# Seven buffers for phase products, halved stores of the last transform, reordered late tiles and W loads spread over the last group

## Chip, cores, metric

One core of one Trainium2 chip runs the kernel. The metric is the device time of one execution in microseconds (us).

## The reference, cut to what matters

```python
def reference(x, h, w_theta, w_tok_r, w_tok_i, w_ch):       # x: 8 x 5696 x 128
    y = irfft(rfft(x, 2 * S) * rfft(h, 2 * S))[:, :S]       # long convolution over the sequence
    theta = y @ w_theta
    zr, zi = y * cos(theta), y * sin(theta)                 # the phase products
    m = einsum('ts,bsd->btd', w_tok_r, zr) + einsum('ts,bsd->btd', w_tok_i, zi)   # W is 5696 x 5696, twice
    u = y + m
    return u + relu(u @ w_ch)
```

The first quarter of the kernel is the convolution, the rest the mixing over the sequence with the two large W matrices. This is about the **handover** between them.

## The kernel before

The convolution runs in eight groups, each in stages A to D. In the last group (stage C from about 408 us, stage D from about 440 us) the phase steps of the first batch half run beside it. The steps of the second half run beside the first mixing products. Each of the 22 steps of a half makes one tile of phase products:

```python
def phase_step(ti, hh):                        # tile ti, batch half hh
    for b in range(4):
        nc.tensor.transpose(tpz[:, b, :], yT[:, b, :], ident_bf)
    if hh:
        y_ap = st["sby"].tile([P, 4, D], BF16, tag="y", name="y_ap")   # 2, later 4 buffers
    else:
        ...                                                            # six slots of "ring"
    def copy():
        nc.vector.tensor_copy(y_ap, tpz)       # ... and a store of y_ap to y2_hbm
    phases_b(ti, y_ap, ...)
    ...
# in phases_b: cos and sin on ScalarE, two products on VectorE, then the stores
zz = fh.tile([P, 2, HD * CK], F16, tag="hs", name="zz")                # four buffers
zi_eng.tensor_mul(zi, red, yflat)
nc.vector.tensor_mul(zr, mag, yflat)
# second half: straight into the operand tiles b of the first mixing pass ("home"), or to z_hbm
(nc.gpsimd if e and r else nc.sync).dma_start(home[j]..., zz[...])
nc.sync.dma_start(z_hbm[...], zz[rows])
```

Of the 11 operand tiles of the first mixing pass, 0 to 8 are home tiles, filled straight from `zz`. Tiles 9 and 10 go through memory: products are stored to `z_hbm` and loaded again after the last step, when the convolution's buffers are free.

```python
def load_b(p, j, pool):
    t_ = tile_b(p, j, pool)
    for z in range(2):
        nc.scalar.dma_start(t_[:, z * 2048:(z + 1) * 2048]..., z_hbm[z, p, j]...)   # ScalarE's queue
```

The steps are called between the first mixing products, which also let further W loads go on GpSimd's queue (`upto` is how many W loads may have been issued, six to begin with):

```python
for q, (h, s) in enumerate(((0, 0), (0, 1), (1, 0), (1, 1))):
    for n in range(4):
        for j in range(TJ):
            product(...)
            if (n * TJ + j) % 2:
                next_steps(1)
        if n % 2 and q < 3:
            ring["upto"] += 1
            pump()
```

Of the kernel before, what the change touches and what calls it, by code (L numbers as in the profile page):

```python
# [22 lines left out]
def kernel(  # L23
# [288 lines left out]

    def stage_c(st):
        sg = sgn[:K1].unsqueeze(2).unsqueeze(1).to_broadcast([K1, 2, N2, 8])

        def chunk(q):
# [9 lines left out]
            g_in = ps[:K1].rearrange("p a (q r n) -> p r n (a q)", q=4, r=2)  # L326
            if q >= 64 and q % 16 == 0:
                nc.scalar.activation(g_out[:, :, :EN], g_in[:, :, :EN], AF.Copy)
                nc.scalar.mul(g_out[:, :, EN:], g_in[:, :, EN:], sgn[:K1, EN:EN + 1])
            else:  # L330
                nc.vector.tensor_tensor(g_out, g_in, sg, op=mult)
        return [lambda q=q: chunk(q) for q in range(0, 2 * HD, 8)]

    def stage_d(st, bp, dh, then=None):
        def chunk(n0, cn):
# [14 lines left out]
            if n0 + cn == N2:  # L350
                if then is not None:
                    then(yt)
                for e in range(2):
                    (nc.gpsimd if then else nc.sync).dma_start(yt_hbm[dh * HD:(dh + 1) * HD, 2 * bp + e, :],
                                                               yt[64 * e:64 * e + 64].rearrange("p m n -> p (m n)"))
        return [lambda n0=n0, cn=cn: chunk(n0, cn) for n0, cn in CHN]

    groups = [(bp, dh) for bp in range(B // 2) for dh in range(2)]

# [14 lines left out]
    def phases_b(ti, y_ap, b0, nb, yT, sb, th_pool, th_tag, zi_eng, turns=None, tags=("red", "mag"), m=P,  # L374
# [36 lines left out]
        if tags is None:  # L411
            zz = fh.tile([P, 2, HD * CK], F16, tag="hs", name="zz").bitcast(BF16)[:, :, :n]
            zr, zi = zz[:, 0], zz[:, 1]
# [7 lines left out]
        for e in range((m + 63) // 64):  # L421
# [7 lines left out]
            if tags is None and j in home:  # L429
                for r in range(2):  # L430
                    (nc.gpsimd if e and r else nc.sync).dma_start(
                        home[j][32 * i:32 * i + 32, :4096].rearrange("p (z q r n) -> p z q r n", z=2, q=2, r=2)[:, :, q_, r],
# [9 lines left out]
    chunks = [(p, tt, c) for p in range(2) for tt in pairs[p] for c in range(len(CHUNKS))]  # L442
    ring = {"n": 0, "read": set(), "wl": 0, "upto": 6}
    loaded = {}
# [57 lines left out]
    def open_phases():  # L502
        st = sides["phases"] = {}
        sb1 = pool("s2", 2, pha, reuse_waits="tile")
        sby = pool("s2y", 2, pha, reuse_waits="tile")
        st["sb1"], st["sby"] = sb1, sby
        sbc = pool("s2c", 1, pha, reuse_waits="tile")
# [40 lines left out]
    def phase_step(ti, hh):  # L548
# [11 lines left out]
        for b in range(4):  # L560
            nc.tensor.transpose(tpz[:, b, :], yT[:, b, :], ident_bf)
        if hh:
            y_ap = st["sby"].tile([P, 4, D], BF16, tag="y", name="y_ap")
        else:
            k = st["n0"] = (st.get("n0", 0) + 1) % 6
            y_ap = ring["all"][:, WB + 4096 + 512 * k:WB + 4608 + 512 * k].rearrange("p (b d) -> p b d", b=4)

# [11 lines left out]
    steps0 = [lambda ti=ti: phase_step(ti, 0) for ti in tile_order]  # L579

    for g, (bp, dh) in enumerate(groups):
        st = {}
        last = g + 1 == len(groups)
        a_, load_, b_ = front(g + 1)
        now = [steps0.pop(0) for _ in range(10)] if last else []
        c_ = stage_c(st)
        if dh == 0 and bp + 1 < B // 2:
# [67 lines left out]
    psp.close()  # L655
    sides["phases"]["sby"] = pool("s2y4", 4, pha, reuse_waits="tile")
    mps = ctx.enter_context(tc.tile_pool(name="mps", bufs=1, space=bass.MemoryType.PSUM, reuse_waits="tile"))
    steps1 = [lambda ti=ti: phase_step(ti, 1) for ti in tile_order]
    bp = cp = wlp = ybp = None
# [219 lines left out]
    for i, (k, p, tt, j0, s0, nj) in enumerate(stretches):  # L879
# [90 lines left out]
        if i == 1:  # L970
# [3 lines that stand above are left out]
                        product((held, a)[s], s * TJ + j, j, n, (h,))  # L974
                        if (n * TJ + j) % 2:
                            next_steps(1)
                    if n % 2 and q < 3:
                        ring["upto"] += 1
                        pump()
# [108 lines left out]
```

## Time and profile before

| | kernel before |
|---|---|
| median, range (4 runs) | 2150.63 us, 2147.27 to 2155.8 us |
| span of the profiled execution | 2155.9 us |
| last group: first product of stage C | 408.45 us |
| first product of stage D | 440.18 us |
| last phase product of the second half ends | 538.12 us |
| twelfth mixing result stored (to `cp_hbm`) | 650.73 us |

These four points cut the handover into three stretches. After the last of them both kernels do the same in the same order.

Timeline of before (columns: start, duration, engine, line and operation, in brackets the idle time before it and what ended it):

```profile
534.06 0.60 ACT L719 ACTIVATE ring<-tpz 128x512 bf16<-128x512 bf16 x1 [1.47 <-PE tpz L717]
540.77 3.42 ACTq L615 DMA_DIRECT2D b<-z_hbm  x4
```

```profile
549.04 3.57 PE L964 MATMUL m<-b,wt 128*128 128x512 bf16 x8 [3.39 <-DMA b<-z_hbm]
...
554.16 4.81 PE L964 MATMUL m<-b,wt 128*128 128x512 bf16 x12 [1.13 <-DMA b<-z_hbm]
```

The four loads stand behind L719, a copy that belongs to a background transposition. The copy is done at 534.7 us, the loads go out from 540.77 us, and TensorE waits 3.39 and 1.13 us for what they bring. Here the copy doesn't hold them: they leave 0.2 us after a store of phase products, issued at 538.15 us, has landed (540.56 us).

### The profile page before, as it was taken

What the parts mean: (1) busy time and instruction counts of PE and PEld (TensorE: products, weight loads), DVE (VectorE), ACT (ScalarE), POOL (GpSimd) and SP (SyncE); (2) the same over time, 40 slices, a digit from 0 to 9 for tenths busy, and PEclk for the clock granted to TensorE, in tenths of its full rate; (3) what the DMA queues carried; (4) which work ended last, traced back from release to release, by engine and by line L of the source; (5) the groups of instructions that cost most, each with busy time, mean ns of one, the idle gap of its engine ahead of it and who ended that gap; (6) DMA issues with size and microseconds to landing.
All of it is one profiled execution on the core that took longest, in us unless ns stands there. A gap on an engine that the chain in (4) does not pass through costs nothing.

```text
span 2155.9 us, 41270 instructions
## 1 busy us (share of the span) xinstructions
PE 2000.3 (93%) x15586; PEld 1124.8 (52%) x15765; DVE 1599.6 (74%) x2884; ACT 674.7 (31%) x992; POOL 889.7 (41%) x1628
## 2 busy tenths in 40 slices
PE   3788889768999999999999997999999999999998
PEld 3787888655444444444444443444444444444444
DVE  7766767766678888788876757578686868686867
ACT  5877868676123232323320000011111111111111
POOL 5211010215435454545556553353535353545351
PEclk8699879999999999999999999999999999999999
DMA  6356473888889998989999879587979797979784
GB/s 138 86 138 162 120 165 99 231 238 221 165 152 174 177 179 168 170 170 177 173 183 153 151 112 309 87 142 125 159 128 155 123 159 129 154 124 159 130 152 91
DMA packets 410695, 335.67 MB, mean 156 GB/s; under 512 B 85927, under 2 KB 361895, under 8 KB 409383
## 3 DMA queue, kind: packets, MB, share of 16 engines
q0 software_dynamic: 224544, 153.24, 50.8%
q1 hardware_dynamic: 178592, 166.02, 26.7%
q10 hardware_dynamic: 7360, 13.76, 1.8%
q8 instruction: 123, 2.02, 0.4%
q14 instruction: 76, 0.62, 0.1%
HBM read 377.11 MB, written 93.21 MB: 218 GB/s over the span
## 4 chain that ended last, share of the span: by engine, by line
PE 64%; DVE 3%; DMA 2%; issue 1%; ACT 0%; POOL 0%; DVEq 0%; ACTq 0%
PE m L1034 58%; PE m L964 2%; DMA b<-z_hbm 2%; DVE c L1041 1%; PE v L776 1%; PE utp L769 1%; PE m L1038 1%; DVE wt L689 1%; PE m L921 1%; PE m L919 1%; PE theta_ps L385 0%; PE tpz L717 0%; DMA yT<-yt_hbm 0%; DMA y_hbm<-ring 0%; POOL ring L493 0%
## 5 line engine op out<-in xcount | busy, mean ns | idle before, releaser
L493 POOL DMA_DIRECT2D ring<-in_moe_w_tok_i_dram x720 | 388.2, 547 | 686.2 <-DVE wt L689 612.1
L493 POOL DMA_DIRECT2D ring<-in_moe_w_tok_r_dram x720 | 386.8, 548 | 240.9 <-PE ps L211 103.5
L689 DVE STREAM_TRANSPOSE wt<-ring 128x384 f32<-128x384 f32 (+2 forms) x720 | 357.9, 522 | 116.3 <-PE m L1034 69.9
L1034 PE MATMUL m<-b,wt 128*128 128x512 bf16 x1604 | 386.6, 381 | 2.9 <-DVE wt L689 0.8
L1034 PEld LDWEIGHTS <-wt 128*128 128x128 bf16 x1804 | 176.6, 98 | 215.7 <-DVE wt L689 3.2
L1041 DVE TENSOR_TENSOR c<-c,m 128x512 f32<-128x512 f32 x412 | 265.1, 669 | 0.4 <-PE m L1034 0.4
L771 ACT ACTIVATE ring<-utp 128x512 bf16<-128x512 bf16 (+1 forms) x86 | 50.9, 592 | 608.6 <-PE utp L769 608.6
L323 PE MATMUL ps<-r_u,u_t 128*128 128x128 f16 x1024 | 133.9, 229 | 15.6 <-DVE u_t L307 12.8
L324 PE MATMUL ps<-r_v,v_t 128*128 128x128 f16 x1024 | 132.7, 228 | 0.0
L964 PE MATMUL m<-b,wt 128*128 128x512 bf16 x469 | 115.6, 393 | 11.4 <-DMA b<-z_hbm 5.8
L766 ACT ACTIVATE ub<-c 128x512 bf16<-128x512 f32 (+1 forms) x90 | 56.3, 628 | 199.1 <-DVE c L935 117.6
L129 POOL DMA_DIRECT2D x<-in_x_dram x64 | 34.1, 538 | 199.3 <-PE ps L193 187.7
L323 PEld LDWEIGHTS <-u_t 128*128 128x128 f16 x1024 | 106.5, 104 | 15.5 <-DVE u_t L307 15.5
L324 PEld LDWEIGHTS <-v_t 128*128 128x128 f16 x1024 | 105.5, 103 | 4.0 <-issue 2.5
L307 DVE TENSOR_TENSOR u_t<-xs,hs 128x1024 f16<-128x1024 f16 x96 | 69.8, 727 | 42.8 <-ACT xs L305 23.8
L305 ACT ACTIVATE xs<-ps 128x1024 f16<-128x1024 f32 x96 | 95.1, 1018 | 18.6 <-DVE v_t L307 10.9
L193 PE MATMUL ps<-f_t,x 89*128 89x180 f16 x512 | 85.0, 313 | 7.2 <-ACT xs L305 4.9
L964 PEld LDWEIGHTS <-wt 128*128 128x128 bf16 x528 | 51.4, 101 | 69.8 <-issue 17.0
L211 PEld LDWEIGHTS <-w_t 64*128 64x128 f16 x3240 | 64.6, 105 | 41.6 <-issue 27.2
L193 PEld LDWEIGHTS <-x 89*128 89x128 f16 x512 | 73.9, 236 | 9.3 <-issue 8.7
L387 ACT ACTIVATE red<-theta_ps,magic 128x512 f32<-128x512 f32 (+1 forms) x46 | 31.6, 687 | 133.5 <-PE theta_ps L385 113.5
L719 ACT ACTIVATE ring<-tpz 128x512 bf16<-128x512 bf16 (+1 forms) x46 | 27.4, 597 | 137.2 <-PE tpz L717 115.8
(2887 smaller groups left out, 3864.4 us busy)
## 6 DMA issues: line engine op xcount, KB each, us to landing
ring<-in_moe_w_tok_r_dram POOLq DMA_DIRECT2D x352, 96.0 KB, 4.5
ring<-in_moe_w_tok_i_dram POOLq DMA_DIRECT2D x352, 96.0 KB, 4.8
ring<-in_moe_w_tok_r_dram POOLq DMA_DIRECT2D x352, 80.0 KB, 4.4
ring<-in_moe_w_tok_i_dram POOLq DMA_DIRECT2D x352, 80.0 KB, 3.8
hs<-hf_hbm SPq DMA_DIRECT2D x192, 128.0 KB, 3.4
cp_hbm<-c SPq DMA_DIRECT2D x88, 256.0 KB, 2.3
c<-cp_hbm SPq DMA_DIRECT2D x88, 256.0 KB, 4.3
out_dram<-c SPq DMA_DIRECT2D x88, 256.0 KB, 4.3
```

What stands on the lines that cost most here:

```text
L193: nc.tensor.matmul(ps[:, i // 2, (i % 2) * 2 * K1:(i % 2 + 1) * 2 * K1], lhs(q + i), f1_t[:NB], start=True, stop=True)
L211: nc.tensor.matmul(ps[:, e, j * HD:(j + 1) * HD], w_t2[rows, c0 + j, N2 * (1 - ri):N2 * (3 - ri)], a_st["a"][rows, ri * K1 + c0 + j, :], s ...
L305: nc.scalar.activation(xs[:, :, :, :ck], ps, AF.Copy)
L307: nc.vector.tensor_tensor(uv[r][:, :, :, c0:c0 + ck], xs[:, :, :, :ck], hv[:, r:r + 1, :, :ck].to_broadcast([P, 2, HD, ck]), op=mult)
L323: nc.tensor.matmul(o, u_t[:, at:at + P], r_u, start=True, stop=False)
L324: nc.tensor.matmul(o, v_t[:, at:at + P], r_v, start=False, stop=True)
L493: nc.gpsimd.dma_start(wb[32 * i:32 * i + 32, :ng, :nj * 64], bass.AP(tensor=a.tensor, offset=a.offset + row0 * S + p * H + i * QR + j0 * 6 ...
L689: nc.vector.transpose(wt.rearrange("p j t r -> p (j t r)").bitcast(F32).rearrange("p (j g t) -> p g j t", j=TJ, g=4)[:, :ng, :nj], wb[:, : ...
L766: nc.scalar.activation(ub[:m].rearrange("p b d -> p (b d)"), c[:m], AF.Copy)
L964: nc.tensor.matmul(ms[n // 2 * 2 + h], a[n][:, j, :, r], bts_of[p][jj][n % 2 * 2 + h][:, r, :], start=(n % 2 == 0 and jj == 0 and r == 0), ...
L1034: nc.tensor.matmul(ms[q], a[q][:, j, :, r], bts[jj][q][:, r, :], start=(jj == 0 and r == 0), stop=(jj == NJ - 1 and r == 1 and q not in left))
L1041: nc.vector.tensor_tensor(c, z, ms[q], op=op)
```

## The change

Its intent is to take the waits out of the handover: more buffers for phase products, another division of their stores between queues, fewer bytes, an earlier start of what comes last. The diff, cut:

```diff
-            if q >= 64 and q % 16 == 0:                       # stage C: evictions on ScalarE
+            if q % 16 == 0 and (last or q >= 64):
...
-                    (nc.gpsimd if then else nc.sync).dma_start(yt_hbm[dh * HD:(dh + 1) * HD, 2 * bp + e, :],
-                                                               yt[64 * e:64 * e + 64].rearrange("p m n -> p (m n)"))
+                    t0 = H if then else 0                     # the last stores: second half only
+                    (nc.gpsimd if then else nc.sync).dma_start(
+                        yt_hbm[dh * HD:(dh + 1) * HD, 2 * bp + e, t0:],
+                        yt[64 * e:64 * e + 64].rearrange("p m n -> p (m n)")[:, t0:])
...
-            zz = fh.tile([P, 2, HD * CK], F16, tag="hs", name="zz").bitcast(BF16)[:, :, :n]
+            k = zz_n[0] = (zz_n[0] + 1) % (4 + ZB)            # ZB = 3: seven buffers
+            zz = (fh.tile([P, 2, HD * CK], F16, tag="hs", name="zz").bitcast(BF16) if k < 4 else
+                  sides["phases"]["zz"].tile([P, 2, 512], BF16, tag="zz", name="zz"))
...
-                    (nc.gpsimd if e and r else nc.sync).dma_start(
+                    (nc.gpsimd if r and (e or zz_n[0] % 2) else nc.sync).dma_start(
...
-    ring = {"n": 0, "read": set(), "wl": 0, "upto": 6}
+    ring = {"n": 0, "read": set(), "wl": 0, "upto": 0}
...                                                            # y_ap: six slots of ring in both halves
+    def with_load(step, load):                                # W loads spread over the last group
+        def both():
+            step()
+            if load:
+                ring["upto"] += 1
+                pump()
+        return both
...
-        now = [steps0.pop(0) for _ in range(10)] if last else []
+        now = [with_load(steps0.pop(0), 2 < n < 9) for n in range(10)] if last else []
...
-    steps1 = [lambda ti=ti: phase_step(ti, 1) for ti in tile_order]
+    steps1 = [lambda ti=ti: phase_step(ti, 1) for ti in
+              [0, 5, 11, 16, 1, 6, 12, 17, 10, 21, 2, 7, 13, 18, 3, 8, 14, 19, 4, 15, 9, 20]]
...
-                    if n % 2 and q < 3:
+                    if n % 2 and q == 1:                      # two calls in place of six
```

More of the change, by code (lines that the diff above doesn't have):

```diff
@@ L311, in stage_b, with stage_c @@
         return [lambda c=c: load(c) for c in range(LEAD)], [lambda c=c: chunk(c) for c in range(NCK)]
-    def stage_c(st):
+    def stage_c(st, last):
         sg = sgn[:K1].unsqueeze(2).unsqueeze(1).to_broadcast([K1, 2, N2, 8])
@@ L353, in chunk @@
                 for e in range(2):
-                    (nc.gpsimd if then else nc.sync).dma_start(yt_hbm[dh * HD:(dh + 1) * HD, 2 * bp + e, :],
-                                                               yt[64 * e:64 * e + 64].rearrange("p m n -> p (m n)"))
+                    t0 = H if then else 0
+                    (nc.gpsimd if then else nc.sync).dma_start(
+                        yt_hbm[dh * HD:(dh + 1) * HD, 2 * bp + e, t0:],
+                        yt[64 * e:64 * e + 64].rearrange("p m n -> p (m n)")[:, t0:])
         return [lambda n0=n0, cn=cn: chunk(n0, cn) for n0, cn in CHN]
+    zz_n, ZB = [0], 3
     groups = [(bp, dh) for bp in range(B // 2) for dh in range(2)]
@@ L504, in open_phases @@
         sb1 = pool("s2", 2, pha, reuse_waits="tile")
-        sby = pool("s2y", 2, pha, reuse_waits="tile")
-        st["sb1"], st["sby"] = sb1, sby
+        st["sb1"] = sb1
+        st["zz"] = pool("s2z", ZB, pha, reuse_waits="tile")
         sbc = pool("s2c", 1, pha, reuse_waits="tile")
@@ L561, in phase_step @@
             nc.tensor.transpose(tpz[:, b, :], yT[:, b, :], ident_bf)
-        if hh:
-            y_ap = st["sby"].tile([P, 4, D], BF16, tag="y", name="y_ap")
-        else:
-            k = st["n0"] = (st.get("n0", 0) + 1) % 6
-            y_ap = ring["all"][:, WB + 4096 + 512 * k:WB + 4608 + 512 * k].rearrange("p (b d) -> p b d", b=4)
+        k = st["n"] = (st.get("n", 0) + 1) % 6
+        y_ap = ring["all"][:, WB + 4096 + 512 * k:WB + 4608 + 512 * k].rearrange("p (b d) -> p b d", b=4)
         def copy():
@@ L584 @@
         a_, load_, b_ = front(g + 1)
-        now = [steps0.pop(0) for _ in range(10)] if last else []
-        c_ = stage_c(st)
+        now = [with_load(steps0.pop(0), 2 < n < 9) for n in range(10)] if last else []
+        c_ = stage_c(st, last)
         if dh == 0 and bp + 1 < B // 2:
@@ L655 @@
     psp.close()
-    sides["phases"]["sby"] = pool("s2y4", 4, pha, reuse_waits="tile")
     mps = ctx.enter_context(tc.tile_pool(name="mps", bufs=1, space=bass.MemoryType.PSUM, reuse_waits="tile"))
-    steps1 = [lambda ti=ti: phase_step(ti, 1) for ti in tile_order]
+    steps1 = [lambda ti=ti: phase_step(ti, 1) for ti in
+              [0, 5, 11, 16, 1, 6, 12, 17, 10, 21, 2, 7, 13, 18, 3, 8, 14, 19, 4, 15, 9, 20]]
     bp = cp = wlp = ybp = None
```

## The prediction

> **What bounds the kernel now.** I read the page first (engine shares, slices), then busy time in stretches of 10 us between 380 and 700 us, then the list of waits for 400 to 680 us, then the timelines of the sync queue, TensorE, VectorE, ScalarE and GpSimd there. The page says that TensorE bounds the kernel nearly everywhere, but that slices 8 to 10 (430 to 590 us; a slice is 53.9 us) are an exception in which the DMA engines are full:
>
> ```profile
> PE 2000.3 (93%) x15586; PEld 1124.8 (52%) x15765; DVE 1599.6 (74%) x2884; ACT 674.7 (31%) x992; POOL 889.7 (41%) x1628
> PE   3788889768999999999999997999999999999998
> DMA  6356473888889998989999879587979797979784
> ```
>
> The diff touches only this handover: the last transform group (about 408 to 457 us), the phase steps of the first batch half (412 to 475 us), those of the second half between the first mixing products (470 to 538 us), and the loads after them. The instruction orders confirm it: TensorE's is the same for its first 14,529 entries and its last 16,063, ScalarE's for its last 492, and GpSimd's differs only between its entries 133 and 207. From 650 to 1200 us TensorE is busy 99.4% or more, so whatever the handover gains moves the rest forward and stays in the total; nothing else can pay.
>
> By stretch (columns: stretch, length, busy TensorE, weight loads, VectorE, ScalarE, GpSimd, granted clock, DMA share, GB/s) TensorE loses time here:
>
> ```profile
> 460.00:470.00 10.00, 1.76 (x17) 1.09 (x16) 4.22 (x9) 5.67 (x11) 0.00 (x0) 0.81 0.99 223
> 470.00:480.00 10.00, 7.49 (x46) 4.68 (x48) 5.37 (x11) 5.24 (x9) 6.02 (x12) 0.68 0.96 289
> 480.00:490.00 10.00, 4.89 (x34) 3.06 (x35) 6.23 (x13) 4.59 (x8) 5.30 (x10) 0.83 1.04 386
> 520.00:530.00 10.00, 6.71 (x42) 3.80 (x41) 5.73 (x11) 6.04 (x11) 3.83 (x7) 0.71 0.77 194
> 540.00:550.00 10.00, 6.55 (x29) 2.85 (x28) 6.37 (x12) 0.00 (x0) 5.54 (x11) 0.91 1.07 238
> ```
>
> The waits (total, times, longest, in us) name the buffers and transfers behind that:
>
> ```profile
> ACT mag L407 <- DVE zz L418: 20.9, 9, 5.2
> DVE zz L417 <- DMA z_hbm<-zz: 14.8, 5, 5.7
> POOL b L626 <- DMA z_hbm<-zz: 13.1, 2, 12.7
> PE tpz L561 <- DMA ya<-yt: 6.9, 2, 5.4
> DVE y_ap L569 <- DMA y_hbm<-y_ap: 5.9, 3, 2.5
> PE m L964 <- DMA b<-z_hbm: 5.8, 4, 3.4
> ```
>
> VectorE waits for the stores of phase products (four buffers), ScalarE waits for VectorE, GpSimd waits for the same stores before it may load operand tiles, and TensorE waits for the transposed input. The sync queue shows why stores are late: it issues without a pause, and slows at the large transfers.
>
> ```profile
> 461.58 2.36 SPq L541 DMA_DIRECT2D ya<-yt  x1
> 464.05 4.92 SPq L435 DMA_DIRECT2D z_hbm<-zz  x2
> 479.45 1.94 SPq L435 DMA_DIRECT2D z_hbm<-zz  x2
> 495.33 27.67 SPq L431 DMA_DIRECT2D b<-zz  x38
> 401.37 2.21 POOL L493 DMA_DIRECT2D ring<-in_moe_w_tok_r_dram  x4 [103.54 <-PE ps L211]
> ```
>
> The first half's last product store is issued at 479 us, although its data stood ready at 475 us; 38 issues in 27.67 us are 0.73 us each.
>
> [...] 0.62 to 0.73 us an issue, three issues a step. [...] 0.68 granted at 470 to 480 us, after a gap of 5.42 us[...].
>
> **The change, part by part.**
>
> *W loads spread over the last group.* It does nothing, I expect. GpSimd has no instruction between the last input load and these 24 issues, in both orders, and the first one waits in both only for TensorE's last read of the old table (the 103.54 us in the last line above). Code that emits them later in the program doesn't make the queue wait. 0 us.
>
> *Half the evictions of the last transform stage on ScalarE.* Before, VectorE does 12 of 1.13 us (start to start) and 10 steps of 1.53 us (0.33 + 0.60 + 0.60): 28.9 us of the 29.6 between 410.6 and 440.2. After: 8 evictions, 24.3 us. ScalarE goes from 10 x 1.66 + 4 x 1.04 = 20.8 to 24.9 us. TensorE needs 16 x 0.90 + 10 x 1.10 = 25.4 us, plus 2 for its slow clock at the start: 27.4 us from 408.45. So TensorE becomes the limit and the next stage starts near 437.7 instead of 440.2: 2.5 us. That next stage is ScalarE's (7 evictions, 5.1 us, and 6 steps, 10.0 us, in 441.2 to 457.3) and only shifts.
>
> *Half of the last stores dropped.* The last two stores carry 64 x 5696 x 2 bytes each, 1.46 MB; now 64 x 2880, 0.74 MB. Between 457 and 472 us 3.29 MB moved at 219 GB/s, so 0.72 MB is 3.3 us. TensorE's wait for `ya<-yt` ended at 470.85; with the 2.5 us it ends near 465.0. Gain so far 5.8 us.
>
> *Seven buffers and six input slots.* From 470.85 to 488.8 us only 3 steps are finished; at the later pace of 2.2 us they take 6.6 us, so some 11 us are lost: VectorE's waits of 4.63 and 2.74 us for stores, TensorE's cold clock, and operand halves that load only once the stores are out. Seven buffers remove the two waits, 7.4 us; but TensorE then meets the operand loads, which must still land, so I count 6. From 488.8 to 522.5 us 15 steps take 2.2 us each, which is the sync queue's pace, 3 issues of 0.73 us. With three of seven buffers sending one more product through GpSimd it is 2.57 x 0.73 = 1.9 us, and TensorE becomes the limit: 1.10 us a step and its share of the 96 products, 96 x 0.216 / 22 = 0.94 us, 2.04 together. 15 x 0.16 is 2 us. The last four steps take 15.7 us (522.5 to 538.1) where 8.8 would do, with VectorE waiting 2.46 us for an input store and 1.56 us for a product store; with six input slots for four I count 4 of the 7.
>
> *Late tiles moved up.* Tiles 10, 21, 4 and 15 feed the two operands that pass through memory. TensorE's waits of 3.39 and 1.13 us for `b<-z_hbm` at 549 and 554 us should shrink by 3. But tiles 9 and 20 now come last and feed operands 7 and 8, which the next products need at once: a landing of about 4 us, less the 1.08 us waited there already, is partly in the open. Net 1 us.
>
> *W loads 8 and 9 later* (two fewer calls in the middle): 8 x 96 KB leave the crowded stretch; already in the above.
>
> Sum: 5.8 + 6 + 2 + 4 + 1 = 18.8 us. 2150.6 - 18.8 = 2131.8 us.
>
> **Rivals.** *DMA-bound.* The DMA share averages 0.92 from 400 to 540 us, with 32.9 MB at 235 GB/s. If bytes are the limit, more buffers only move the wait, and the gain is what leaves: 0.72 MB and 0.79 MB of W, 6.4 us: 2144 us. For it: shares near 1. Against it: other stretches move 289 and 386 GB/s, and shares of 0.70, 0.76, 0.77 and 0.53 (440 to 460, 520 to 540 us) show slack. *Full repair.* If the backlog of stores disappears, operand tiles come early too, all the lost 11 and 7 us return, and both waits for `b<-z_hbm` go: 5.8 + 11 + 2 + 7 + 4.5, about 30 us: 2120 us. *W late.* W loads 10 to 13 landed 14.5 us after their issue (538.8 to 553.3 us); if the phases end 18 us sooner but W takes as long and starts with two loads still open, the second tile pair waits up to 5 us (my estimate): 2137 us. Or the sums of operand 0, which overwrite the input slots, hold VectorE for the last input stores.
>
> **Range and chances.** The rivals span 2120 to 2144 us, and I take that as the range, with the sum of the parts in its middle. A gain over 2% needs 43 us; TensorE's idle time in the stretches from 410 to 570 us adds up to 32 us, so hardly 2 in 100. A loss of 43 us has no mechanism here.
>
> **What would show it.** Right: no wait of VectorE for `zz` stores before the second half's steps; `ya<-yt` ending near 465 us; first half's last product store issued before 472 us; about 2.05 us a step in the middle; the W loads still first issued at about 401 us; the stretch from 700 us on unchanged but shifted by about 19 us. Wrong: W issued later; DMA share at 1 with the same waits under other names; a new long wait of TensorE for `b<-zz` or W after the last step.

The 2 us for a slow clock at the start of stage C are an estimate from TensorE's timeline: the granted clock is 0.55 from 408.45 to 411.94 us and 1.00 from there to 420 us. "TensorE's cold clock" is the 0.68 granted at 470 to 480 us. "A landing of about 4 us" is that of the home stores, whose median from issue to landing is 4.2 us on the sync queue and 4.1 us on GpSimd's (405 to 560 us).

## More of the kernel before

A run that is one look only has one time, so I compare such runs by landmarks inside their profiles and not by their times.

Busy time in the stretches of before (columns: stretch, length, busy TensorE, its weight loads, VectorE, ScalarE, GpSimd, each with its number of instructions, then the clock granted to TensorE as a share of full speed, the busy share of the DMA engines, and GB/s):

```profile
408.45:440.18 31.73, 27.13 (x391) 24.36 (x397) 28.56 (x42) 21.31 (x38) 8.13 (x15) 0.95 1.08 276
440.18:538.12 97.94, 75.20 (x705) 49.69 (x719) 62.49 (x117) 65.10 (x111) 40.74 (x74) 0.90 0.88 228
538.12:650.73 112.61, 103.52 (x490) 47.73 (x499) 81.18 (x151) 27.92 (x46) 42.96 (x80) 0.92 0.82 159
```

Length minus busy TensorE is its idle time: 4.60, 22.74 and 9.09 us, together 36.4 us. That is all that a better handover could give, beyond a faster clock.

## The result

| | before | changed |
|---|---|---|
| median (4 runs each) | 2150.63 us | 2147.85 us |
| range | 2147.27 to 2155.8 us | 2143.98 to 2149.52 us |
| ratio, 95% interval | | 0.9982, 0.9958 to 1.0007 |
| span of the profiled execution | 2155.9 us | 2147.7 us |

A ratio is the mean time of one kernel's runs over that of the other's of the same rounds, so it isn't quite the ratio of the medians. The class is "same", as predicted. The time isn't: 2147.85 us lies above the range of 2120 to 2144 us.

In the page's slices (TensorE, DMA) of the changed kernel, counted from 0, TensorE's weakest slice (8, about 430 to 483 us) has risen from 6 to 7, and slice 10 (537 to 590 us) has fallen from 9 to 8:

```profile
PE   4788889778899999999999998999999999999998
...
DMA  6356473889779898999999879686969696879684
```

Of the stretches that the prediction showed, these answer in the changed kernel:

```profile
460.00:470.00 10.00, 4.42 (x33) 3.05 (x32) 8.62 (x17) 8.15 (x15) 3.14 (x6) 0.66 0.99 235
...
480.00:490.00 10.00, 6.44 (x54) 3.90 (x54) 5.38 (x10) 5.49 (x10) 6.88 (x13) 0.97 1.00 340
...
540.00:550.00 10.00, 5.79 (x18) 2.12 (x17) 1.68 (x4) 1.17 (x2) 3.46 (x7) 0.70 0.89 210
```

The head of the second half is better filled (4.42 and 6.44 us busy against 1.76 and 4.89), but 540 to 550 us is worse: 5.79 against 6.55 us, at a lower granted clock (0.70 against 0.91), and now the phase steps are long over there. The waits between 436 and 560 us (total, times, longest):

```profile
ACT ring L729 <- PE tpz L727: 13.4, 1, 13.4
...
DVE zz L422 <- ACT red L411: 12.8, 21, 1.4
...
PE m L974 <- DMA b<-z_hbm: 8.7, 4, 4.2
...
DVE ring L641 <- DMA y_hbm<-ring: 5.8, 1, 5.8
DVE ring L571 <- DMA y_hbm<-ring: 5.8, 3, 3.3
```

VectorE no longer waits for stores of phase products (14.8 us before) but for ScalarE, step by step. Its wait for the stores of transposed inputs (L571, the former L569) is as large with six slots as before (5.8 and 5.9 us); it now lies at 478 to 488 us and no longer at 508 to 525. TensorE's wait for operand tiles through memory has grown from 5.8 to 8.7 us. The wait in the first line has grown from 1.5 us. L641 is new: VectorE builds sums in the memory of the input slots and waits 5.8 us for their last stores, as the prediction's last rival said it might. No wait of TensorE behind it shows in this profile. The sync queue and GpSimd's first W loads in the changed kernel:

```profile
460.39 1.95 SPq L546 DMA_DIRECT2D ya<-yt  x1
...
474.55 1.81 SPq L440 DMA_DIRECT2D z_hbm<-zz  x2
...
498.43 16.41 SPq L436 DMA_DIRECT2D b<-zz  x22
```

```profile
398.93 2.21 POOL L498 DMA_DIRECT2D ring<-in_moe_w_tok_r_dram  x4 [101.41 <-PE ps L211]
```

The first half's last product stores went out from 474.55 us instead of 479.45; the predicted 472 was not reached. The queue still needs 16.41 / 22 = 0.75 us an issue. The W loads start as early as before, not spread at all.

The three stretches of the changed kernel:

```profile
407.54:437.72 30.18, 26.92 (x390) 24.28 (x397) 23.87 (x37) 25.62 (x46) 7.63 (x14) 0.94 1.08 277
437.72:521.05 83.33, 69.97 (x691) 47.83 (x704) 62.95 (x118) 64.96 (x110) 41.21 (x76) 0.92 0.90 246
521.05:641.65 120.60, 106.28 (x505) 48.50 (x514) 81.34 (x151) 28.53 (x47) 45.59 (x86) 0.94 0.83 158
```

Up to the last phase product it gains 1.55 + 14.61 = 16.2 us; then it gives 7.99 us back. Over all, 242.3 us have become 234.1. TensorE's idle time by stretch is 3.26, 13.36 and 14.32 us, together 30.9 instead of 36.4. The third stretch is where it got longer, by 5.2 us. The rest of what is given back is 2.8 us of TensorE's work, 15 recorded matmuls (490 and 505), that stood before the last phase product and now stand behind it.

What fills the third stretch is told by ScalarE's timeline of the changed kernel, then TensorE's:

```profile
532.36 0.60 ACT L729 ACTIVATE ring<-tpz 128x512 bf16<-128x512 bf16 x1 [13.35 <-PE tpz L727]
532.58 9.42 ACTq L625 DMA_DIRECT2D b<-z_hbm  x4
```

```profile
526.19 5.91 PE L974 MATMUL m<-b,wt 128*128 128x512 bf16 x18 [2.10 <-DMA b<-zz]
531.94 0.39 PE L727 MATMUL tpz<-ident_bf,yT 128*128 128x128 bf16 x4
...
538.52 1.89 PE L974 MATMUL m<-b,wt 128*128 128x512 bf16 x7 [2.10 <-DMA b<-z_hbm]
...
545.90 5.19 PE L974 MATMUL m<-b,wt 128*128 128x512 bf16 x12 [4.21 <-DMA b<-z_hbm]
```

The copy L729 waits 13.35 us for its transposition L727. That stands in TensorE's stream behind mixing products which wait for a home tile until 526.19 us. The four loads of tiles 9 and 10 stand behind the copy in ScalarE's queue, and the first two leave as soon as it has started. The last two (538.91 and 541.63 us) are held by something else, which act_order below shows; TensorE's longer wait, until 545.90 us, is for the third. So the phase steps end 17.1 us sooner (521.05 against 538.12), but the first of these loads goes out only 8.2 us sooner, and TensorE waits for them twice, 6.3 us in all, where it waited 4.5 us before.

### The profile page after: what moved, and what is told of

The parts are those of the page before. It is cut to its first block, busy times and chain, and to the rows that moved or that the text cites. A ratio compares the mean times of both kernels' runs of the same rounds, so it can differ in the third digit from the quotient of the medians. Undisturbed runs are those within 1.5% of the kernel's fastest.

```text
span 2147.7 us, 41283 instructions
## 1 busy us (share of the span) xinstructions
PE 1996.8 (93%) x15587; PEld 1121.7 (52%) x15765; DVE 1595.9 (74%) x2880; ACT 677.4 (32%) x1000; POOL 892.7 (42%) x1634
## 4 chain that ended last, share of the span: by engine, by line
PE 61%; DMA 3%; DVE 2%; issue 1%; POOL 1%; ACT 0%; DVEq 0%; ACTq 0%; POOLq 0%
PE m L1044 55%; PE m L974 2%; DMA b<-z_hbm 2%; POOL ring L498 1%; DVE c L1051 1%; PE v L786 1%; PE utp L779 1%; PE m L1048 1%; DMA ring<-in_moe_w_tok_r_dram 1%; DMA wl<-in_moe_w_tok_i_dram 1%; DVE wt L699 1%; PE m L931 1%; PE m L929 1%; DMA ring<-in_moe_w_tok_i_dram 0%; PE tpz L727 0%
## 5 line engine op out<-in xcount | busy, mean ns | idle before, releaser
L729 ACT ACTIVATE ring<-tpz 128x512 bf16<-128x512 bf16 (+1 forms) x46 | 27.4, 597 | 152.1 <-PE tpz L727 130.3
```

## The experiments

I made 18 more runs, two of them repeats: the twelve of the first three batches and six more because the cause was still open. The measure is the time between landmarks, in us. "C to D" is from the first product of the last group's stage C to the first of stage D, "D to product" from there to the end of the last phase product, "to result 12" from there until the twelfth mixing result is stored, and "whole" is the sum. "D to product" repeats within 1.6 us in the two pairs of equal kernels, "whole" within 2.8 us, so a difference in "whole" below 3 us says nothing. Each row is one profile.

| kernel | C to D | D to product | to result 12 | whole |
|---|---|---|---|---|
| before | 31.7 | 97.9 | 112.6 | 242.3 |
| before_again | 32.9 | 96.4 | 110.2 | 239.5 |
| changed | 30.2 | 83.3 | 120.6 | 234.1 |
| after_again (changed) | 30.6 | 82.6 | 118.8 | 232.0 |
| act_order | 30.0 | 83.8 | 115.9 | 229.7 |
| load_pool | 30.0 | 84.0 | 111.6 | 225.6 |
| four_bufs | 33.2 | 85.4 | 123.3 | 241.9 |
| full_store | 30.0 | 87.9 | 123.8 | 241.7 |
| dve_evict | 32.2 | 82.3 | 120.1 | 234.7 |
| old_order | 31.1 | 82.6 | 118.8 | 232.5 |
| no_split | 31.0 | 82.9 | 117.5 | 231.4 |
| four_nosplit | 31.0 | 88.1 | 115.6 | 234.7 |
| four_nosplit_slots4 | 30.4 | 85.9 | 117.3 | 233.6 |
| old_order_pool | 30.2 | 82.7 | 112.1 | 225.0 |
| pump3 | 31.4 | 83.8 | 114.0 | 229.3 |
| before_pump1 | 32.2 | 91.3 | 110.0 | 233.4 |
| before_half | 32.3 | 92.1 | 110.5 | 234.8 |
| before_half_pump1_pool | 32.6 | 88.4 | 108.5 | 229.5 |
| pump3_pool | 30.1 | 85.7 | 115.1 | 230.8 |
| before_pool | 33.0 | 97.6 | 105.6 | 236.1 |

My first theory after the result was **L**: what is given back comes from the late loads of tiles 9 and 10. The rival **R** was that something else binds there (the DMA engines, or a granted clock like the 0.70 of 540 to 550 us).

### after_again and before_again: how much is scatter

No edit; both kernels once more.

> The changed kernel once more, unaltered, for a ratio from more rounds and a second profile. In the first pair of profiles the changed one ends 8.1 us sooner, but the timed medians differ by 2.8 us only. Theory A: the 8.1 us are the change's and the first timing hid them in scatter; then the ratio comes out near 0.996 (8 us). Theory B: the first profile of the kernel before was a long execution (its run took 2157.6 us against a median of 2150.6); then the ratio is near 0.9985 (3 us), and a second profile of before will be shorter by several us outside the handover. In both the span from the start of the last group's stage D to the last phase product of half 1 is 83 us, and the stretch from there to the start of the fourth ScalarE copy of the first pair's results is 30 us.

> The kernel before once more, one look, for a second profile. By theory A its landmarks repeat within 1 us (last phase product of half 1 at 538 us, fourth copy of the first pair at 560 us, end at 2156 us). By theory B the last phase product still lies 97 to 98 us after the start of stage D of the last group, but the end is at 2147 to 2152 us, and the shift against the first profile arises gradually or in a place that has nothing to do with the handover.

after_again: median 2146.23 us of 6 runs (2139.11 to 2158.77) beside 2153.73 us of 11 runs of before; ratio 0.9975, interval 0.9949 to 1.0001. By the means the change is worth 2153.3 - 2147.5 = 5.7 us here and was worth 3.8 us in the first runs. The handover says 240.9 - 233.1 = 7.8 us, from two profiles each. Both theories of the expectation were too simple. The handover's gain does repeat. But before's second span is 2149.5 us against 2155.9: its stage C began 1.75 us sooner, its handover took 2.8 us less and the rest 1.8 us less. That is scatter spread over the whole execution, which is as large as the effect.

### act_order: ScalarE in program order at the head of the mixing

```diff
-            ordered.enter_context(tc.manual_schedule(engines={mybir.EngineType.DVE}))
+            ordered.enter_context(tc.manual_schedule(engines={mybir.EngineType.DVE} | ({mybir.EngineType.Activation} if p == 0 else set())))
```

> The changed kernel with ScalarE kept in program order over the first stretches of the mixing, so that the four loads of operand tiles 9 and 10 stand directly behind the last phase step in ScalarE's queue, ahead of the copy of a background transposition for which they wait 13.35 us in the changed kernel. Theory L (the 9 us given back after the last phase product are the late loads of tiles 9 and 10): the loads are issued at 522 to 529 us, the TensorE waits of 2.10 and 4.21 us on them at 538 and 546 us are gone or below 1 us, the fourth copy of the first pair starts at 543 to 547 us in place of 551.4, and the end moves by 5 to 8 us against the changed kernel, ratio to before 3 us lower or more. Rival R (the products after the last phase step are bound by something else: by the transfer engines, which the W loads fill, or by the cold clock): the loads go out sooner but land only 1 to 2 us sooner, and the end moves by less than 2 us.

Median 2141.64 us, ratio 0.9951 (0.9932 to 0.9969). ScalarE's and TensorE's timeline:

```profile
522.66 14.39 ACTq L625 DMA_DIRECT2D b<-z_hbm  x4
```

```profile
540.97 1.89 PE L974 MATMUL m<-b,wt 128*128 128x512 bf16 x8 [2.35 <-DMA b<-z_hbm]
...
544.20 1.02 PE L974 MATMUL m<-b,wt 128*128 128x512 bf16 x4 [1.34 <-DMA b<-z_hbm]
```

The first load went out 9.9 us sooner, and the copies of the first pair's results (four in all) began at 545.48 instead of 551.35 us, as L expected of what it calls the fourth; the mean time fell from 2147.5 to 2142.3 us. (With six runs each, and 2139.11 to 2158.77 us in the changed kernel, that difference alone isn't clear of scatter.) But the waits didn't vanish (3.7 us are left), because the four loads took 14.39 us to leave the queue. L holds in direction, and R's bound of 2 us is passed.

What spaced the four loads out is in the packed trace, which keeps the semaphores that each instruction waits for and each transfer reports on. In this program the transfers of the sync queue and of ScalarE's queue share eight semaphores (111 to 118; in the changed kernel 1,052 and 28 transfers report on them), and those of GpSimd's queue have eight of their own (101 to 108; 1,596 transfers). Each of these loads first waits until the last transfer on its semaphore has landed. Loads 2, 3 and 4 left at 528.59, 532.78 and 536.69 us, right after transfers of the sync queue had landed on theirs: a home store at 528.57 us, and two loads of `yT` for the background at 532.61 and 536.67 us, issued 9.6 and 12.8 us before. In the changed kernel the third and fourth load leave at 538.91 and 541.63 us in the same way, after the store of the copied tile (landed on semaphore 117 at 538.74 us) and a load of `yT` (on 118 at 541.61 us). So the copy holds two of the four loads, and transfers that have nothing to do with tiles 9 and 10 hold the others.

### load_pool: the same loads on GpSimd's queue

```diff
-            nc.scalar.dma_start(
+            (nc.scalar if p else nc.gpsimd).dma_start(
                 t_[:, z * 2048:(z + 1) * 2048]...
```

> The changed kernel with the loads of operand tiles 9 and 10 issued from GpSimd's queue instead of ScalarE's, everything else as it is. It tests theory L in another way, for ScalarE's order stays as it is. Theory L: the loads no longer wait for the ScalarE copy; they are issued when their data are there (522 to 529 us) unless W loads in front of them in that queue hold them, and the end moves by 3 to 8 us. Rival R: less than 2 us. If the W loads in front hold them the loads go out after 530 us, the gain is nil, and the run tells nothing against theory L.

Median 2143.67 us, ratio 0.9958 (0.9939 to 0.9976). GpSimd's timeline:

```profile
525.43 3.19 POOL L625 DMA_DIRECT2D b<-z_hbm  x4 [0.56 <-DMA ring<-in_moe_w_tok_i_dram]
```

All four loads left in 3.19 us, on GpSimd's semaphores, TensorE has no wait for them any more, and "to result 12" is 111.6 us, as short as before's. The whole handover is 7.5 us shorter than the changed kernel's mean of 233.1. So the late loads are shown in two ways. But this edit also takes them off the semaphores of the sync queue, and before_pool below shows that not all of its gain is the release from the copy.

### four_bufs, full_store, dve_evict, old_order: one part undone

```diff
-    zz_n, ZB = [0], 3
+    zz_n, ZB = [0], 0                      # four_bufs (its pool of three goes too)
-                    t0 = H if then else 0
+                    t0 = 0                 # full_store
-            if q % 16 == 0 and (last or q >= 64):
+            if q >= 64 and q % 16 == 0:    # dve_evict
-              [0, 5, 11, 16, 1, 6, 12, 17, 10, 21, 2, 7, 13, 18, 3, 8, 14, 19, 4, 15, 9, 20]]
+              tile_order]                  # old_order
```

> The changed kernel with four buffers for the phase products again in place of seven, all else as changed. Judged by the span from the start of the last group's stage D to the last phase product of half 1, which repeats within 1.5 us (97.9 and 96.4 us in two profiles of before, 83.3 and 82.6 in two of the changed kernel). Theory of the prediction (seven buffers give 6 us in the start transient, 2 in the middle and some of the last four steps): 90 to 94 us, and VectorE again waits for stores of phase products. Rival (the buffers are worth little once the W loads and the large stores are out of the way, so most of the 14 us is the half stores' and the queue split's): below 86 us.

> The changed kernel with the whole of the last transform's tiles stored again, all else as changed. Theory of the prediction (the half stores free the queues in front of the second half's first loads: 3.3 us): stage D to last phase product is 86 to 87 us instead of 83, and TensorE waits for the second half's operand (ya from yt) again. Rival (hidden): within 1 us of 83.

> The changed kernel with the evictions of the last group's stage C as before (VectorE alone in its first half), all else as changed. Theory of the prediction: the span from the first product of the last stage C to the first of stage D is 32.2 us (31.7 and 32.9 before; 30.2 and 30.6 changed), so 2 us longer, and the rest stays: 83 us from stage D to the last phase product. Rival: the 2 us are taken up by the waits at the head of the second half, so stage D to the last phase product shrinks by as much as stage C grows.

> The changed kernel with the second half's steps in the old order (tiles 10 and 21, which operand tiles 9 and 10 need, last again). Theory L (in the changed kernel the loads of operand tiles 9 and 10 stand behind a ScalarE copy until 532 us anyway): the new order is worth next to nothing there, so last phase product to fourth copy of the first pair stays at 30 us, within 3. Rival (the order is worth the 3 us and more that the prediction gave it): 33 us or more from the last phase product to that copy, and the loads wait for the stores of the phase products.

**four_bufs** took 85.4 us from stage D to the last product. That is below 86, so the rival is right there: three more buffers are worth 2.5 us there, though VectorE does wait 10.5 us for `zz` stores again. (Its stage C took 2.8 us longer too, 3.0 us of VectorE's waits there being for `zz` stores; the two other runs with four buffers don't show that, 31.0 and 30.4 us.) **full_store** took 87.9 us, a little more than the predicted 86 to 87, and TensorE waits 4.1 us for `ya` again: the half stores are worth some 5 us in that stretch. **dve_evict** added 1.8 us to stage C, and the next stretch was 0.6 us shorter than the changed kernel's mean; the theory of the prediction holds in size (TensorE waits for `ya` in this run too, 5.0 us, so that wait alone doesn't tell the store's effect). **old_order** came out at 232.5 us, like the changed kernel. The number is what theory L expected, but the run doesn't test its reason: here the scheduler put the copy behind the loads, and the first load left at 534.57 us, when the store of a late tile's products, issued at 527.52 us, had landed (534.55 us). Late data and a free queue came to the same as early data and a blocked one; old_order_pool below is the cleaner test.

Two wholes, 241.9 and 241.7 us, are larger than these parts explain. In both the copy stands ahead of the loads and the loads begin at 532.2 and 536.1 us, but so it does in dve_evict (532.0 us), whose whole is 234.7 us. In no_split, four_nosplit, four_nosplit_slots4, old_order and pump3 the scheduler put the copy behind the loads. The same edit thus also moves that copy, and a whole that differs by a few us can't be put down to the edited part alone.

### no_split, four_nosplit, four_nosplit_slots4: the buffer part undone piece by piece

```diff
-                    (nc.gpsimd if r and (e or zz_n[0] % 2) else nc.sync).dma_start(
+                    (nc.gpsimd if e and r else nc.sync).dma_start(        # in all three
# four_nosplit: ZB = 0 as well; four_nosplit_slots4: the pools of two and four for y_ap as well
```

> The changed kernel with every second product's store on the sync queue again (seven buffers, but the old division: one of four home stores on GpSimd, three on sync), all else as changed. Theory S (the pace of the middle steps, 2.2 us before and 1.97 us changed, is the sync queue's three issues of 0.73 us): the middle steps take 2.15 to 2.25 us again, whatever the number of buffers, and stage D to last phase product is 86 to 88 us in place of 83. Rival B (the seven buffers carry the pace by themselves): 1.97 us a step and 83 to 84 us.

> The changed kernel with four buffers and the old division of the stores, all else as changed. Four buffers alone gave 85.4 us from stage D to the last phase product, against 83. If the division and the buffers each take their own wait away, this one is about 89 us (83 + 2.5 + 3.5). If they stand in for each other (slow issues only hurt because four buffers run out), it is well above 90 us, near the 96 to 98 us of before.

> The changed kernel with the whole buffer part undone: four buffers for phase products, old division of their stores, and the transposed inputs of the second half in the old pools of two, later four, in place of six slots. Left of the change: evictions, half stores, order of the late tiles, two fewer W loads in the middle. By the prediction (buffers, slots and division 12 us of its sum) stage D to last phase product is 93 to 97 us. If it is 3 us or more above the run with four buffers and the old division, the six slots carry that; if it is equal, the slots are worth nothing.

no_split kept the pace of 1.97 us a step (from 502 to 514 us) and 82.9 us: theory S, that the sync queue's issue time sets the pace, fell. four_nosplit took 88.1 us, near the 89 of independent waits. With the slots undone as well it took 85.9 us, far below the 93 to 97 that the prediction implies. Its three stretches, last two rows:

```profile
438.44:524.31 85.87, 69.94 (x688) 48.11 (x701) 62.61 (x117) 65.62 (x111) 40.38 (x73) 0.90 0.90 240
524.31:641.58 117.27, 105.61 (x507) 48.78 (x517) 81.38 (x151) 28.54 (x47) 43.50 (x81) 0.96 0.82 162
```

TensorE's idle time over the handover is 3.1 + 15.9 + 11.7 = 30.7 us, the same as with everything (30.9 and 31.2). Buffers, slots and division together are worth 2.9 us up to the last product (116.3 against a mean of 113.4) and nothing to the twelfth result (233.6 against 233.1). In these three runs the copy stands behind the loads, and the first load leaves at 530.9, 528.2 and 528.4 us. The third still leaves only at 535.2 to 539.0 us, after loads of `yT` on the shared semaphores have landed, and TensorE waits 4.4, 7.8 and 7.5 us for the loads. Taking the copy away is thus not enough. The six slots were not undone alone beside seven buffers; no run shows that case.

That the pace was never the queue's can be read off the middle stretch, before and then changed:

```profile
490.00:515.00 25.00, 24.79 (x214) 15.54 (x217) 18.59 (x34) 19.01 (x34) 18.73 (x34) 1.00 0.95 222
```

```profile
490.00:515.00 25.00, 24.79 (x216) 15.85 (x219) 20.50 (x39) 21.30 (x37) 20.88 (x39) 0.94 0.96 239
```

TensorE was busy 24.79 of 25 us there already before the change. What the two kernels do with it differs: more steps in the same busy time leave less of it to the mixing products.

### old_order_pool: old order, loads on GpSimd

The edits of old_order and load_pool together.

> The changed kernel with the second half's steps in the old order and the loads of operand tiles 9 and 10 on GpSimd's queue. With the ScalarE queue, old and new order came out alike (from the first product of the last stage C to the twelfth stored result 232.5 us with the old order, 234.1 and 232.0 with the new). With GpSimd's queue and the new order it was 225.6 us. Theory L2 (the new order pays only once the loads don't stand behind the ScalarE copy): 228 to 232 us here, with waits of 2 us or more for operand tiles through memory. Rival (the order is worth nothing in either case): 225 to 227 us.

225.0 us, so the rival is right: even with the loads free the new order is worth nothing that I can measure. The loads then left at 530.5 us instead of 525.4, after 4.2 us of waiting for `z_hbm` stores, and the one wait of TensorE for them was 1.43 us. The later start is made up elsewhere.

### pump3, before_pump1, before_half, before_half_pump1_pool: the bytes

By then the 14 us up to the last product were without a cause, so I turned to what the prediction had counted as "already in the above". By its own working the two calls fewer keep 0.79 MB of W out of the middle.

```diff
-                    if n % 2 and q == 1:
+                    if n % 2 and q < 3:                  # pump3, on the changed kernel
-                    if n % 2 and q < 3:
+                    if n % 2 and q == 1:                 # before_pump1, on the kernel before
# before_half: the halved stores alone on the kernel before
# before_half_pump1_pool: both, and load_b on GpSimd as in load_pool, on the kernel before
```

> The changed kernel with four W loads let go in the middle of the second half's steps (tiles 6 to 9) as before, in place of two, all else as changed. Theory D (the handover is bound by the transfer engines, so what counts is which bytes stand in it, not how many buffers wait for them): the middle steps take 2.2 us or more again instead of 1.97, and stage D to last phase product is 88 to 91 us in place of 83; to the twelfth stored result it is 1 to 4 us more than the 232 to 234 of the changed kernel. Rival P (the W loads fit into idle time of the transfer engines, and the pace came from six slots and the order of tiles): 83 to 85 us.

> The kernel before with nothing changed but that: two W loads let go in the middle of the second half's steps in place of four. Theory D: the middle steps take 2.0 us in place of 2.5, and stage D to last phase product is 90 to 93 us in place of 96 to 98. Rival P: 95 us or more.

> The kernel before with nothing changed but the last transform's stores halved. Theory D: 0.72 MB at 220 to 240 GB/s leave the head of the second half, so stage D to last phase product is 3 to 5 us shorter, 92 to 94 us, and the pace of the middle steps stays at 2.5 us. Rival P (what the store held up is then held up by the four buffers): 96 us or more.

> The kernel before with three edits only: halved stores, two W loads in the middle in place of four, and the loads of the operand tiles through memory on GpSimd's queue. Four buffers, old slots, old division of stores, old evictions, old order of tiles. By theory D the rest of the change is worth nearly nothing: first product of the last stage C to twelfth stored result 226 to 230 us (before 239.5 and 242.3, changed with GpSimd's loads 225.6), and the median is within 4 us of the 2143.7 us of that one. Rival P (buffers, slots and evictions are needed for it): 232 us or more and a ratio to before above 0.998.

On the kernel before, either edit alone comes out where theory D said: 91.3 and 92.1 us from stage D to the last product in place of 97.2, and 233.4 and 234.8 us as a whole in place of 240.9. **That one line of the change, or the halved stores alone, gives most of what the whole change gives** (7.5 and 6.0 of 7.8 us, one profile each). Theory D's reason isn't shown for the line, though. The middle steps should have taken 2.0 us; the 18th product ends at 522.4 us, as before (522.5), and the gain lies in the last four steps, 8.7 us in place of 15.7 and 12.1. Nor do W loads 6 to 9 leave the stretch: they go out at 500.8 to 528.6 us instead of 495.0 to 518.2 (497.3 to 522.1 in the changed kernel), so they move by some microseconds and are all still issued ahead of the last product (531.1 us). On the changed kernel, pump3 misses: undoing the same line costs only 0.9 us from stage D to the last product, and the whole gets 3.8 us shorter. The scheduler now put the copy behind the loads, they went out from 525.14 us, and TensorE has no wait for them:

```profile
525.14 7.69 ACTq L625 DMA_DIRECT2D b<-z_hbm  x4
```

before_half_pump1_pool, with four buffers, old slots, old division, old evictions and old order, comes to 229.5 us, within the 226 to 230 expected of theory D, and to a median of 2144.53 us, ratio 0.9954 (0.9939 to 0.9968). That is as good as load_pool's 0.9958 and act_order's 0.9951.

### pump3_pool and before_pool

The edits of pump3 and load_pool on the changed kernel; that of load_pool alone on the kernel before.

> The changed kernel with four W loads in the middle as before and the loads of operand tiles 9 and 10 on GpSimd's queue. Four W loads alone gave 229.3 us from the first product of the last stage C to the twelfth stored result, because there the scheduler put the four loads in front of the ScalarE copy and they went out from 525 us; GpSimd's queue alone gave 225.6 us. Theory L (both act through the same cause, the time at which tiles 9 and 10 land): the two don't add, 224 to 228 us and a median within 3 us of 2143.7. Rival (W landing earlier is a gain of its own): 222 us or less, median 2140 or less.

> The kernel before with nothing changed but the queue of the loads of operand tiles 9 and 10: GpSimd in place of ScalarE. In the profile of before these loads wait for the stores of the last phase products (issued 6.5 us after the ScalarE copy), not for the copy. Theory L: so the repair alone gains nothing there, 239 to 243 us from the first product of the last stage C to the twelfth stored result. Rival (the ScalarE queue holds the loads in both kernels alike, so the repair is worth its 6 to 8 us in either): 232 to 236 us.

Both miss their numbers. pump3_pool: median 2143.72 us, ratio 0.9959 (0.9937 to 0.9981), 230.8 us as a whole, so the gains don't add; it is even 5 us above load_pool, and I don't know why. before_pool gives 236.1 us, between the two theories. GpSimd's timeline there:

```profile
539.07 1.46 POOL L615 DMA_DIRECT2D b<-z_hbm  x2 [0.88 <-DMA z_hbm<-zz]
...
541.40 1.41 POOL L615 DMA_DIRECT2D b<-z_hbm  x2 [0.88 <-issue]
```

The loads go out no sooner than before (540.8 us), yet TensorE waits 1.46 us for them instead of 4.52. So load_pool's gain has two parts. One is the release from the copy, which only the changed kernel needs and which act_order alone shows as 3.4 us (233.1 to 229.7). The other, 4 to 5 us, comes with GpSimd's queue even where the loads start no sooner. There the loads land 5.7 to 7.6 us after their issue, where before took 8.2 to 11.1 us and its second profile 6.9 to 12.5. They stand ahead of the next W loads, and the trace shows these waiting until they have landed (3.3 us in before_pool, 6.8 us in load_pool); that this is why they land sooner is argued and not shown.

**Not run.** A kernel with the W spread undone compiles to the same instruction streams, with the same waits, as the changed kernel: no difference in 31,532 entries of TensorE, 1,030 of ScalarE, 2,882 of VectorE, 1,639 of GpSimd and 1,054 of the sync engine. That part of the change does nothing, and no run is needed to say so. Raising the loads' scheduling priority, and moving them to the sync queue, left them behind a ScalarE instruction in the order that was built; I didn't run those either, and no trace shows them.

**The best versions** are act_order (2141.64 us), load_pool (2143.67 us), pump3_pool (2143.72 us) and before_half_pump1_pool (2144.53 us). Their means are 2142.3, 2143.2, 2143.8 and 2144.3 us against 2147.5 of the changed kernel and 2152.5 to 2154 of before. Each is clear of the kernel before by its interval; the order among the four is within scatter.

## Why the prediction was wrong

**W loads spread: 0 us.** Right; the instruction streams are identical.

**Evictions on ScalarE: 2.5 us.** Right in kind and nearly in size: C to D shrank by 1.9 us on the mean of two profiles, and undoing it cost 1.8 us. That stage D began at 437.72 us, where 437.7 was predicted, is luck: the prediction's own sum, 27.4 us from 408.45, ends at 435.9, and stage C began 0.9 us sooner than in before. TensorE was busy 26.92 of 30.18 us there, so it was near to being the limit, with 3.26 us idle.

**Half of the last stores: 3.3 us.** Right in mechanism, mis-sized: 5.1 us from stage D to the last product on the kernel before and 4.9 us in the changed one. The landmark held: the transfer `ya<-yt` landed at 465.97 us (predicted near 465; 470.80 before). TensorE's wait there (5.43 us) is now booked on ScalarE, whose last step of the first half ended at 465.60 us, so both came nearly together.

**Seven buffers and six slots: 6, 2 and 4 us.** This is the first step that failed. VectorE's waits for `zz` vanished, as predicted, but undoing buffers, slots and division together costs 2.9 us up to the last product and 0.5 us to the twelfth result. The start was gained and given back: from the landing of `ya<-yt` to the third product the changed kernel takes 9.9 us, before 18.0 and four_nosplit_slots4 22.5; the fifteen steps after it take 35.8, 33.7 and 29.5 us. The 2 us of a quicker middle never came (33.7 and 34.3 us before, 35.8 and 33.2 changed). VectorE's waits for buffers are now those for the stores of the six slots (L571, 5.8 us), which the slots should have taken away; the DMA-bound rival had said that more buffers only move the wait. The "later pace of 2.2 us" was read as "the sync queue's pace, 3 issues of 0.73 us", though TensorE was busy 24.79 of 25 us in that stretch. The prediction showed the stretches at 460 to 490 and at 520 to 550 us, where TensorE has holes, and not the one between them.

**W loads 8 and 9 later, "already in the above".** Also wrong: alone on the kernel before, this is worth 5.9 us from stage D to the last product, as much as any part. (The line drops four calls of six, not two; in the traces loads 6 to 9 still go out in this stretch, later.) Half stores, W loads, evictions and buffers, each measured by itself, give 5.1 + 5.9 + 1.9 + 2.9 = 15.8 us; the whole change gave 16.1 us up to the last product (129.5 to 113.4, means of two), and the prediction's parts without the last one came to 17.8. So the sum up to there came out nearly right with the wrong owners. It isn't strictly additive: undone in the changed kernel, the W edit costs 0.9 us.

**Late tiles moved up: the waits for `b<-z_hbm` "should shrink by 3", net 1 us.** This is the step that failed most. They grew, from 4.5 to 6.3 us, and the stretch behind the last product grew from 111.4 to 119.7 us, means of two. The prediction asked when the data of tiles 9 and 10 would be ready, and not what else their loads wait for in ScalarE's queue: a copy (until 532.36 us for loads 1 and 2), and landings of sync-queue transfers on the shared semaphores (538.74 and 541.61 us for loads 3 and 4). What stands before a load in its own queue, and what that load itself waits for, it looked up for the W loads only. The new order itself is worth nothing measurable in either form.

**The sum.** 18.8 us were expected at the end. The handover lost 7.8 us, and the timed means 3.8 and 5.7 us. Every microsecond gained before the last phase product was booked as gained at the end, but half of it went into TensorE's idle time and unfinished products behind that point. Of the rivals, the DMA-bound one came nearest in time (2144 us) and named the two edits that carry most (halved stores and later W loads, to it bytes that leave). It is not shown as stated: act_order and load_pool move no byte fewer and still gain 5.3 and 4.4 us of mean time over the changed kernel. The rival of full repair failed, and with it the lower end of the range. One reading at its start was too strong as well: the slices that it calls full of DMA show 8 tenths, and of its three exceptions TensorE's third slice shows 9.

**What stays open:** why four_bufs and full_store lose some 8 us as a whole when their own part explains 3 to 5, why two calls in place of six shorten the last four steps on the kernel before, and why pump3_pool isn't as good as load_pool.

## What to carry to other kernels

When a phase is made to end sooner, follow what must start at its end, transfer by transfer: its data, what stands ahead of it in its queue, and the semaphore that it waits for. In this case it was the data before the change: a store that landed at 540.56 us, and the first load left at 540.77 us. In the changed kernel a compute instruction, the copy that started at 532.36 us, set the first two loads (532.58 and 533.00 us), and background transfers of another queue, landed at 538.74 and 541.61 us, the last two (538.91 and 541.63 us). Before you credit buffers with the pace of a stretch, look at the busy time of the bounding engine in exactly that stretch: here 24.79 of 25 us, and VectorE's 10.5 us of waits for buffers in four_bufs made the stretch only 2.5 us longer. And in a crowded handover parts stand in for each other, so test each alone on the old kernel and undone in the new one, and don't add their gains: 6.0 us (halved stores), 7.5 us (W loads) and 4.7 us (GpSimd's queue), each alone on the kernel before, gave 11.4 us together, by the means of before's two profiles.
